# Query weights of a decode attention kernel: 448 rows spread evenly, 64 rows placed by DMA engine

## The chip, the cores and the metric

The kernel runs on one core of a Trainium2 chip. A core has TensorE (PE, with weight loads shown as PEld), VectorE (DVE), ScalarE (ACT), GpSimd (POOL) and SyncE (SP, which here only issues transfers), each with its own instruction queue run in order, and 16 DMA engines that move data between HBM and the on-chip memory of 128 partitions (SBUF). SP, ACT and POOL can issue DMAs; each queue's transfers are spread over the 16 DMA engines. The metric is device time in microseconds, the median of several runs.

## The reference: what is computed

One decode step, all in float32: a layer norm of `x`, a query projection, attention of 8 batches and 32 query heads over 8 cached key/value heads of 8192 positions, an output projection, and beside it a token-mixing MLP; the three are added.

```python
B, Sq, D = 8, 1, 512
Hq, Hkv, Sk, Dh = 32, 8, 8192, 128
xn = _layernorm(x, axis=-1)
q = (xn @ wq).reshape(B, Sq, Hq, Dh)            # wq: (512, 4096), 8.4 MB
k, v = repeated k_cache, v_cache                # each (8, 8, 8192, 128), 268 MB
p = softmax(q k^T * Dh ** -0.5)
attention = (p v).reshape(B, Sq, Hq * Dh) @ wo  # wo: (4096, 512), 8.4 MB
h = _layernorm(xn, axis=-1)
mixer = gelu(h * w1 + b1) summed over 1792 features with w2, + b2
out = x + attention + mixer
```

## The kernel before, in words

Caches and weights come to 553.7 MB, read once. They pass through a ring of five slots (`slots`, 32 KB per partition each, 4 MB in all per slot). `slot(n)` hands out the next n slots in turn. `load_next()` takes the next load of a fixed list: first the key and value heads of kv-head pairs (`load_duo`, 8 MB each: K0, V0, K1, V1, ... with i = pair and batch), then, from kv head 6 on, one head of one batch at a time (4 MB). All these loads are issued on SP's queue in that order; each waits until the slots it overwrites have been read. A load that spans slots 4 and 0 is issued as two transfers (V0 is the first such).

The order of work within an engine is the order of the program (`manual_schedule`); waits on semaphores between engines, and between a transfer and whoever reads or overwrites its target, are put in by the framework. Transfers from SP and ACT share eight completion counters in turn, those from POOL eight others: a transfer waits for the one that used its counter before it.

Start: `load_wq` (L88) reads all of `wq` into slots 0 and 1 as one transfer, four weight rows (64 KB) per partition. `load_next()` then issues K0 into slots 2 and 3 in four pieces and, after it, V0, whose first half goes into the free slot 4 and whose second half needs slot 0 and so the end of the projection. POOL issues `w1`, `b1`, `w2` and `b2` (L158 to L161), makes the identity matrix and clears `Z`, `PT` and `OTS` (L248 to L257). DVE builds small constant masks from the identity (L171 to L246; `fill_softmax`, `fill_place`, with scratch space in `early`), then does the layer norms and `yx = x + b2` into `macc` (L277), which waits for `b2`'s transfer. PE transposes `xn` (L282), puts `yx` into its place (L285), and then `q_project` (L297) does 32 matmuls: each group of four writes four 32-row groups of one PSUM tile. ACT copies the result, PE transposes it (L303), DVE stores it as `QT`.

Main loop (`duo_step`): DVE transposes the keys in place in 32x32 blocks (L480), PE forms scores (L491), a softmax runs over DVE, PE and ACT, and PE multiplies with the values (L523). Two halves of K are done one after the other; the first half's last matmul frees its slot, and `load_next()` issues the next K there. `load_wo(0)` is issued in step i = 2.

Of the kernel before, what the change touches and what calls it, by code (L numbers as in the profile page):

```python
# [10 lines left out]
ALU = mybir.AluOpType  # L11
# [29 lines left out]
PAD = 384  # L41


@with_exitstack
def attn_mixer_kernel(ctx: ExitStack, tc: tile.TileContext, x, kc, vc, wq, wo, w1, b1, w2, b2, out):
# [38 lines left out]
    WQ = []  # L84

    def load_wq():
        t = slot(2).rearrange("p s m -> p (s m)")
        nc.sync.dma_start(t, wq.rearrange("(p c) n -> p (c n)", c=NC))  # L88
        t = t.rearrange("p (c n) -> p c n", c=NC)
        WQ.extend(t[:, c, :] for c in range(NC))  # L90
# [57 lines left out]
    load_wq()  # L148
    early = one.tile([P, HB, 512], F32, name="ob")
    x_sb = early[:B, 0, :]  # L150
    nc.scalar.dma_start(x_sb, x.rearrange("b s d -> (b s) d"))
# [3 lines left out]
    b2t = const.tile([B, 1], F32, name="b2t")  # L155
    yrow = const.tile([W, D], F32, name="yrow")
    load_next()
    nc.gpsimd.dma_start(w1t, w1.rearrange("s (p c) -> p (s c)", p=P))  # L158
    nc.gpsimd.dma_start(b1t, b1.rearrange("(p c) -> p c", p=P))
    nc.gpsimd.dma_start(w2t, w2.rearrange("(p c) s -> p (c s)", p=P))  # L160
    nc.gpsimd.dma_start(b2t, bass.AP(tensor=b2.tensor, offset=b2.offset, ap=[[0, B], [1, 1]]))  # L161
# [3 lines left out]
    ident = const.tile([P, P], F32, name="ident")  # L165
    make_identity(nc, ident)

    oh32 = pad[:, 3 * NF:3 * NF + W]  # L170
# [19 lines left out]
    def fill_softmax(duo, tmp):  # L190
        tmp = tmp[:, :P]
        n = 2 if duo else 1
        rows = tmp[:, :n * REP].rearrange("p (s h) -> p s h", h=REP)
        nc.vector.tensor_reduce(rows, ident.rearrange("p (c s x h) -> p s h c x", c=NCH, s=n, h=REP), AX.XY, ALU.add)
        for s in range(n):
            nc.vector.tensor_scalar(hmask.rearrange("p (c s x h) -> p s c x h", c=NCH, s=n, h=REP)[:, s],
                                    rows[:, s].unsqueeze(1).unsqueeze(1).to_broadcast([P, NCH, B // n, REP]),
                                    1.0, 3.0e38, op0=ALU.subtract, op1=ALU.mult)
        if duo:
            nc.vector.memset(send, 0.0)  # L200
            for k in range(2):
                for a in range(NB):
                    o = a * W + a // 2 * HW
                    nc.vector.tensor_copy(send[:, k, o:o + HW].rearrange("p (c h) -> p c h", h=REP),
                                          ident.rearrange("p (c x h) -> p c x h", c=NCH, h=REP)[:, :, 2 * a + k, :])
        else:
            nc.vector.tensor_copy(send[:, 0, :].rearrange("p (x c h) -> p c x h", c=NCH, h=REP),
                                  ident.rearrange("p (c x h) -> p c x h", c=NCH, h=REP))

    def fill_place(duo, tmp):  # L210
        tmp = tmp[:, :P]
# [24 lines left out]
    fill_softmax(True, early[:, 2, :])  # L236
    fill_place(True, early[:, 3, :])
    epst = const.tile([B, 1], F32, name="epst")
    nc.vector.memset(epst, EPS)
# [8 lines left out]
    nc.gpsimd.memset(Z, 0.0)  # L248
    PT = []
    for k in range(NPT):  # L250
        t = const.tile([P, CH_T * W + W], F32, name=f"pt{k}")
        nc.gpsimd.memset(t, 0.0)
        PT.append(t)
    OTS = []
    for k in range(2):
        t = const.tile([P, REP, W], F32, name=f"ot{k}")
        nc.gpsimd.memset(t, 0.0)  # L257
        OTS.append(t)


    def layer_norm(dst, src):
        st = work.tile([B, 6], F32, name="st")
        nc.vector.bn_stats(st, src)
        mv = work.tile([B, 2], F32, name="mv")
        nc.vector.bn_aggr(mv, st)
        sd = work.tile([B, 1], F32, name="sd")
        nc.scalar.activation(sd, mv[:, 1:2], AF.Sqrt, bias=epst)
        rs = work.tile([B, 1], F32, name="rs")
        nc.vector.reciprocal(rs, sd)
        nc.vector.tensor_scalar(dst, src, mv[:, 0:1], rs, op0=ALU.subtract, op1=ALU.mult)  # L270

    xn = early[:B, 1, :]
    layer_norm(xn, x_sb)
# [4 lines left out]
    xnT = early[:, 2, P:2 * P].rearrange("p (c b) -> p c b", b=W)  # L278
    nc.vector.memset(xnT, 0.0)
    m = misc()  # L280
    for c in range(NC):
        nc.tensor.transpose(m[:, c * B:(c + 1) * B], xn[:, c::NC], ident[:B, :B])  # L282
    nc.vector.tensor_copy(xnT[:, :, :B], m[:, :NC * B].rearrange("p (c b) -> p c b", b=B))
# [7 lines left out]
    def q_project():  # L291
        for a in range(2):
            m = misc()
            for c in range(NC):
                for g in range(HKV // 2):
                    o = (a * HKV // 2 + g) * REP * DH
                    nc.tensor.matmul(m[g * W:(g + 1) * W, :], xnT[:, c, :], WQ[c][:, o:o + REP * DH],  # L297
                                     start=(c == 0), stop=(c == NC - 1))
# [3 lines left out]
            for r in range(REP):  # L302
                nc.tensor.transpose(mt[:, r * P:(r + 1) * P], q[:, r * DH:(r + 1) * DH], ident)  # L303
            nc.vector.tensor_copy(QT[:, a * HKV // 2:(a + 1) * HKV // 2].rearrange("p g b r -> p r g b"),
                                  mt.rearrange("p (r g b) -> p r g b", r=REP, b=W)[:, :, :, :B])
        WQ.clear()
# [293 lines left out]
    def duo_step(i):  # L600
# [27 lines left out]
        if b == 2:  # L628
# [150 lines left out]
```

## Time and profile before

| What | Value |
|---|---|
| median of 3 runs | 1292.99 us (1292.84 to 1293.36) |
| the profiled execution | 1293.02 us, span 1291.2 us |
| busy: PE, DVE, ACT, POOL | 923.2, 701.6, 233.0, 229.5 us |
| moved by DMA | 554.41 MB, mean 429 GB/s |
| first and last of 40 slices | 399 and 322 GB/s |
| chain that ended last | DMA 59%, PE 20%, DVE 19% |
| granted TensorE clock | 0.879 of full speed |

Times in the profile are in us from the span's start; a row of the timeline has start, duration, engine, line, operation, target and sources, and in brackets the idle time before it and what ended it. Rows of the chain of waits have start, duration and what the time went to. In rows of issues the last number is the time from issue to landing. The engine shown as SPq or ACTq is the queue that issues.

### The profile page before, as it was taken

The numbers are of one execution on the slowest core, as the hardware profiler recorded it, in microseconds if no ns is written. First come the engines' busy times: TensorE is split into PE (matmuls) and PEld (weight loads), VectorE is DVE, ScalarE is ACT, GpSimd is POOL, SyncE is SP. The second block draws the span as 40 slices with busy tenths as digits, with TensorE's granted clock in tenths as the row PEclk, the third lists the DMA queues.
The fourth block names the chain that finished last, engine by engine and source line by source line (L and its number), as shares of the span: only waits on it lengthen the run. The fifth ranks groups of instructions, "written<-read, shape, count | busy, mean of one in ns | idle before, by whom it ended". The sixth has DMA issues, their size and how long they took to land.

```text
span 1291.2 us, 11170 instructions
## 1 busy us (share of the span) xinstructions
PE 923.2 (72%) x4742; PEld 246.7 (19%) x4742; DVE 701.6 (54%) x581; ACT 233.0 (18%) x346; POOL 229.5 (18%) x247
## 2 busy tenths in 40 slices
PE   2766865866885876886768787688688674665778
PEld 0211211211221111211112121122112111111223
DVE  3544635644655633665445665346565745566575
ACT  0112220122121122121221221211222332310000
POOL 1022220222031222111221212211223311100000
PEclk9978997988998889898889988799897887878889
DMA  9999999999999999999999999999999999999997
GB/s 399 445 425 447 423 431 443 425 435 435 432 436 433 421 441 439 425 434 441 422 444 425 427 445 418 435 442 429 427 437 428 432 434 431 432 436 429 433 436 322
DMA packets 15925, 554.41 MB, mean 429 GB/s; under 512 B 1884, under 2 KB 1916, under 8 KB 2692
## 3 DMA queue, kind: packets, MB, share of 16 engines
q1 hardware_dynamic: 15732, 553.67, 99.4%
q8 instruction: 37, 0.61, 0.2%
q14 instruction: 12, 0.10, 0.0%
q0 software_dynamic: 128, 0.02, 0.0%
q10 hardware_dynamic: 16, 0.02, 0.0%
HBM read 553.69 MB, written 0.02 MB: 429 GB/s over the span
## 4 chain that ended last, share of the span: by engine, by line
DMA 59%; PE 20%; DVE 19%; ACT 1%; issue 1%; POOL 0%; SPq 0%; DVEq 0%; ACTq 0%; POOLq 0%
DMA raw<-in_A_k_cache_dram 54%; DVE raw L480 14%; PE acc L491 10%; DMA raw<-in_A_v_cache_dram 4%; DVE raw L336 3%; PE acc L414 3%; PE acc L523 3%; DMA b2t<-in_B_b_dram 2%; PE acc L347 1%; PE misc L511 1%; PE misc L297 1%; PE misc L540 1%; DVE mr L359 0%; ACT t2k L508 0%; DVE mr L500 0%
## 5 line engine op out<-in xcount | busy, mean ns | idle before, releaser
L491 PE MATMUL acc<-raw,z 128*32 128x512 f32 x1536 | 401.1, 642 | 188.6 <-DVE raw L480 183.2
L480 DVE STREAM_TRANSPOSE raw<-raw 128x2048 f32<-128x2048 f32 x192 | 424.1, 2274 | 170.8 <-DMA raw<-in_A_k_cache_dram 170.8
L575 POOL TENSOR_SCALAR g<-g,pad 128x512 f32<-128x512 f32 x112 | 77.5, 692 | 753.0 <-ACT g L574 753.0
L491 PEld LDWEIGHTS acc<-raw,z 128*32 128x32 f32 x1536 | 92.0, 116 | 496.4 <-issue 317.8
L523 PE MATMUL acc<-raw,pt 128*32 128x512 f32 x1536 | 181.5, 610 | 5.2 <-DMA raw<-in_A_v_cache_dram 5.2
L336 DVE STREAM_TRANSPOSE raw<-raw 128x2048 f32<-128x2048 f32 x64 | 145.6, 2293 | 60.7 <-DMA raw<-in_A_k_cache_dram 60.7
L576 POOL TENSOR_TENSOR macc<-macc,g 128x512 f32<-128x512 f32 x112 | 142.1, 1269 | 9.3
L574 ACT ACTIVATE g<-hb,pad 128x512 f32<-128x512 f32 x112 | 87.2, 778 | 147.6 <-POOL macc L576 125.4
L508 ACT ACTIVATE t2k<-acc,nb 128x512 f32<-128x512 f32 x24 | 16.5, 687 | 462.4 <-DVE nb L504 462.3
L347 PE MATMUL acc<-raw,z 128*32 128x512 f32 x512 | 82.2, 645 | 10.6 <-DVE raw L336 7.9
L511 PE MATMUL misc<-t2k,send 128*128 128x512 f32 x96 | 62.4, 785 | 33.5 <-ACT t2k L508 33.5
L414 PE MATMUL acc<-raw,pt 128*32 128x512 f32 x480 | 79.6, 803 | 0.0
L523 PEld LDWEIGHTS acc<-raw,pt 128*32 128x32 f32 x1536 | 48.0, 113 | 137.4 <-issue 106.7
L512 DVE STREAM_TRANSPOSE pt<-misc 128x512 f32<-128x512 f32 x48 | 34.4, 717 | 69.4 <-PE misc L511 67.7
L500 DVE TENSOR_REDUCE mr<-acc 128x1 f32<-128x512 f32 x24 | 16.6, 691 | 89.1 <-PE acc L491 89.1
L364 PE MATMUL misc<-ident,mr 128*128 128x128 f32 x16 | 6.5, 406 | 74.0 <-DVE mr L359 74.0
L574 ACT ACT_TABLE_LOAD x32 | 41.1, 1283 | 26.6 <-PE hb L566 26.1
L531 ACT COPY ob<-acc 128x512 f32<-128x512 f32 x24 | 14.0, 584 | 133.1 <-PE acc L523 133.1
L381 ACT ACTIVATE t2k<-acc,nb 128x512 f32<-128x512 f32 x16 | 11.0, 687 | 133.9 <-DVE nb L370 133.8
L347 PEld LDWEIGHTS acc<-raw,z 128*32 128x32 f32 x512 | 19.4, 116 | 62.7 <-issue 43.5
L636 ACT ACT_TABLE_LOAD x24 | 30.8, 1283 | 0.4
L540 PE MATMUL misc<-ob,pick 128*128 128x512 f32 x64 | 29.5, 603 | 0.4 <-ACT ob L531 0.4
(119 smaller groups left out, 334.6 us busy)
## 6 DMA issues: line engine op xcount, KB each, us to landing
raw<-in_A_k_cache_dram SPq DMA_DIRECT2D x26, 4096.0 KB, 28.6
raw<-in_A_v_cache_dram SPq DMA_DIRECT2D x25, 4096.0 KB, 28.1
raw<-in_A_k_cache_dram SPq DMA_DIRECT2D x4, 2048.0 KB, 33.3
wo<-in_A_wo_dram SPq DMA_DIRECT2D x7, 1024.0 KB, 28.8
raw<-in_A_v_cache_dram SPq DMA_DIRECT2D x3, 1024.0 KB, 21.8
raw<-in_A_v_cache_dram SPq DMA_DIRECT2D x2, 512.0 KB, 25.4
wo<-in_A_wo_dram SPq DMA_DIRECT2D x4, 256.0 KB, 16.3
raw<-in_A_v_cache_dram SPq DMA_DIRECT2D x19, 28.8
```

What stands on the lines that cost most here:

```text
L336: nc.vector.transpose(k, k)
L347: nc.tensor.matmul(S[i][c * W:(c + 1) * W, :].rearrange("p (t j) -> p t j", j=W), Z[:, q, b, REP:], k[:, c * CH_T:(c + 1) * CH_T, q * W:(q ...
L414: nc.tensor.matmul(O[i][j * W:(j + 1) * W, :].rearrange("p (c d) -> p c d", c=NCH), pt[:, t * W:(t + 1) * W], v[:, t], start=(t < NB), sto ...
L480: nc.vector.transpose(k, k)
L491: nc.tensor.matmul(SD[i][c * W:(c + 1) * W, :].rearrange("p (t j) -> p t j", j=W), Z[:, q, b, (1 - k) * REP:(1 - k) * REP + W], t[:, c * C ...
L511: nc.tensor.matmul(m, send[:, k, :], p, start=True, stop=True)
L512: nc.vector.transpose(PT[k][:, :CH_T * W], m)
L523: nc.tensor.matmul(OD[i][j * W:(j + 1) * W, :].rearrange("p (c d) -> p c d", c=NCH), PT[k][:, t * W:(t + 1) * W], v[:, t], start=(not k an ...
L540: nc.tensor.matmul(m.rearrange("p (b d) -> p b d", b=HB), pick[:, c, :], ob[:, :, c * DH:(c + 1) * DH], start=(c == 0), stop=(c == NCH - 1))
L574: nc.scalar.activation(g, hb, AF.Gelu_apprx_tanh, bias=b1t[:, j:j + 1], scale=w1t[:, j:j + 1])
L575: nc.gpsimd.tensor_scalar(g, g, w2t[:, j:j + 1], 1.0, op0=ALU.mult, op1=ALU.mult)
L576: nc.gpsimd.tensor_add(acc, acc, g)
```

## The change: what it does

The 512 rows of `wq` are no longer one transfer. The first 448 rows (D - WS with WJ = 14) lie as 14 pieces of 4 KB in each of the 128 partitions: `body`, 56 KB per partition in slots 0 and 1, loaded in two halves. The last 64 rows (WS), 16 KB each, go to chosen partitions of slot 4 (`extra`), one or two rows side by side (WE = 2); all else in `extra` is filled with zeros by DVE (3072 columns), POOL (2560) and ACT (2560) beforehand. [...] SP issues 28 of these rows and the last 16 columns of six and of four half rows; POOL issues the rest in six transfers with six dummy transfers of a few bytes between them (`pass_over`), one ahead of each.

Since a partition now holds pieces of different rows, `xn` is laid out to match: DVE copies it into `xg` and `xs` (42 small copies), PE transposes, DVE scatters the result into `lw` and `lx`, zero elsewhere. `q_project` has 44 matmuls instead of 32: 14 on the first half of `body`, 16 on `extra`, 14 on the second half.

Moved along: `x` and `b2` are issued first, on ACT's queue; `w1`, `b1`, `w2` are issued by POOL after the rows; `load_wo(0)` follows K0 on SP's queue; `Z`, `PT`, `OTS` are cleared by DVE; the scratch space of `fill_softmax` and `fill_place` moves from `early` to the rest of slot 1 (`spare`), as `lw` and `lx` now lie in `early`. V0 still goes to slots 4 and 0.

```diff
+    flat = wq.rearrange("d n -> (d n)")
+    body = slot(2).rearrange("p s m -> p (s m)")
+    extra = slots[:, RING - 1, :]
+    rows = flat[:P * WJ * WB].rearrange("(p m) -> p m", p=P)
+    half = WJ // 2 * WB
+    nc.sync.dma_start(body[:, :half], rows[:, :half])
+    spare = body[:, WJ * WB:]
+    nc.vector.memset(nil, 0.0)
+    nc.vector.memset(extra[:, :3072], 0.0)
+    nc.gpsimd.memset(extra[:, 3072:5632], 0.0)
+    nc.scalar.copy(extra[:, 5632:], nil.to_broadcast([P, WE * DR - 5632]))
...
+    def load_block(eng, p, n, r, d, hop, m=1):
+        to = extra[p:p + n * r, :m * DR].rearrange("p (e c) -> p e c", c=DR)
+        eng.dma_start(to, from_wq(d, [hop * DR, n], [DR, r * m]))
+        given.extend((p + i * r, r, d + i * hop, m) for i in range(n))
+
+    def load_steps(eng, p, step, n, d, hop, m=2, skip=1):
+        to = extra[p:p + (n - 1) * step + 1:step, :m * DR].rearrange("p (e c) -> p e c", c=DR)
+        eng.dma_start(to, from_wq(d, [hop * DR, n], [skip * DR, m]))
...
+    def pass_over(n):
+        at = 3 * NF + W + passed[0] // 2 * 4 + passed[0] % 2
+        passed[0] += 1
+        nc.gpsimd.dma_start(pad[:n, at:at + 3:2].unsqueeze(2), wq[:n, 0:3:2].unsqueeze(2))
+
+    D0 = D - WS
+    load_block(nc.sync, 0, 5, REP, D0, 6)
+    load_steps(nc.sync, W, REP, 3, D0 + 4, 6)
+    load_steps(nc.sync, W + 1, REP, 2, D0 + 60, 1, 1)
...
+    load_top(nc.sync, slice(DR - 16, DR))
+    load_halves(nc.sync, DR // 2 - 16, 16)
+    nc.sync.dma_start(body[:, half:WJ * WB], rows[:, half:])
+
+    def load_side():
+        pass_over(7)
+        load_block(nc.gpsimd, 60, 2, REP, D0 + 30, 10, 2)
+        pass_over(6)
+        load_top(nc.gpsimd, slice(0, DR - 16))
...
+        pass_over(7)
+        load_steps(nc.gpsimd, 28, 68, 2, D0 + 22, 1, 2, 6)
+        pass_over(6)
+        load_steps(nc.gpsimd, W + 2, 92, 2, D0 + 38, 1, 2, 13)
+        pass_over(6)
+        load_halves(nc.gpsimd, 0, DR // 2 - 16)
...
+        pass_over(6)
+        load_steps(nc.gpsimd, W + 3, 92, 2, D0 + 56, 1, 2, 2)
...
     load_next()
+    load_wo(0)
+    ident = const.tile([P, P], F32, name="ident")
+    make_identity(nc, ident)
+    load_side()
...
-    fill_softmax(True, early[:, 2, :])
-    fill_place(True, early[:, 3, :])
+    fill_softmax(True, spare[:, 7 * P:7 * P + HP])
+    fill_place(True, spare[:, 7 * P + HP:8 * P])
...
-    nc.gpsimd.memset(Z, 0.0)
+    nc.vector.memset(Z, 0.0)
...
+        part = [[(lw[:, j, :], body[:, j * WB:(j + 1) * WB]) for j in range(a * WJ // 2, (a + 1) * WJ // 2)] for a in range(2)]
+        part.insert(1, [(lx[:, j, :], extra[:, j * WB:(j + 1) * WB]) for j in range(WE * NB)])
...
-        if b == 2:
+        if g and b == 2:
             load_wo(2 * g)
```

What the built programs hold at three places. Names in brackets are the semaphores that the instruction waits for: DMAHW0 to 7 are the completion counters of transfers from SP and ACT, DMASW0 to 7 those from POOL, used in turn.

SP's queue at the start, now (before, row L88 and K0's four pieces stood first, without a wait, and V0's first half behind them, without a wait too):

```order
L100 DMA raw<-in_A_wq_dram 128x7168
L115 DMA raw<-in_A_wq_dram 20x1x4096 [waits DVE_49,Pool_49]
L120 DMA raw<-in_A_wq_dram 3x8192 [waits Activation_49]
L143 DMA raw<-in_A_wq_dram 128x7168 [waits DMAHW0_49]
L175 DMA raw<-in_A_k_cache_dram 128x4096 [waits DMAHW1_49]
L215 DMA wo<-in_A_wo_dram 128x2048 [waits DMAHW5_49]
L181 DMA raw<-in_A_v_cache_dram 128x8192 [waits DMASW7_49,DMASW5_49,DMAHW6_49,DMASW3_49,DMAHW7_49,DMASW1_49,PE_49]
L181 DMA raw<-in_A_v_cache_dram 128x8192 [waits DMAHW0_49,PE_49]
```

V0's first half (the first L181) now waits for PE, up to its last matmul on `extra`.

DVE, from the constants to the projection, before:

```order
L181 COPY rep<-ident 128x512
L194 TENSOR_REDUCE ob<-ident 128x8
L196 TENSOR_SCALAR hmask<-ob 128x4x16 [waits DVE_49]
L277 TENSOR_SCALAR macc<-ob,b2t 8x512 [waits DMASW3_49]
L304 COPY qt<-misc 128x4x32 [waits PE_49] x2
```

and now:

```order
L294 COPY rep<-ident 128x512
L306 TENSOR_REDUCE raw<-ident 128x8 [waits DMAHW4_49,DMASW7_49,DMAHW5_49,DMASW5_49,DMASW1_49]
L308 TENSOR_SCALAR hmask<-raw 128x4x16 [waits DVE_49]
L357 MEMSET z 128x1152
L361 MEMSET pt_257 128x544
L373 TENSOR_SCALAR macc<-ob,b2t 8x512 [waits DMAHW2_49]
L401 COPY qt<-misc 128x4x4x8 [waits PE_49] x2
```

The scratch space now lies in the ring's memory, and the framework makes its first write (L306) wait for transfers of rows into other places of that memory. DMASW1 is raised by POOL's block (`load_block`) and again by its half rows (`load_halves`); L306 waits for both.

PE around the projection, now, with POOL's own queue behind it:

```order
L375 MATMUL misc<-macc,ob 32x512 [waits DVE_49]
L391 MATMUL misc<-raw,ob 32x512 [waits DMAHW1_49]
L391 MATMUL misc<-raw,ob 32x512 x6
L391 MATMUL misc<-raw,ob 32x512 [waits DMAHW3_49,DMASW7_49,DMAHW4_49,DMASW5_49,DMAHW5_49,DMASW3_49,DMASW1_49]
```

```order
L126 DMA pad<-in_A_wq_dram 7x2x1
L115 DMA raw<-in_A_wq_dram 8x1x8192 [waits DVE_49,Activation_49]
L126 DMA pad<-in_A_wq_dram 6x2x1 [waits DMASW0_49]
L139 DMA raw<-in_A_wq_dram 2x2x2032 [waits DMASW1_49]
```

As before, the matmul on `macc` (L375, was L285) stands ahead of the projection, and `macc` waits for all of DVE's rows above it. POOL's half rows (L139) wait until its block has landed, since they use the same counter.

More of the change, by code (lines that the diff above doesn't have):

```diff
@@ L41 @@
 PAD = 384
+WJ = 14
+WB = 2 * REP * DH
+WS = D - P * WJ // NB
+WV = 2
+WE = 2
 @with_exitstack
@@ L83, in attn_mixer_kernel @@
     order[at], order[at + 1] = order[at + 1], order[at]
[L84 to L90, printed above, removed]
+    early = one.tile([P, HB, 512], F32, name="ob")
+    x_sb = early[:B, 0, :]
+    nc.scalar.dma_start(x_sb, x.rearrange("b s d -> (b s) d"))
+    b2t = const.tile([B, 1], F32, name="b2t")
@@ new lines, in attn_mixer_kernel @@
+    xn = early[:B, 1, :]
+    layer_norm(xn, x_sb)
+    cls = const.tile([P, WV], F32, name="cls")
+    nc.vector.tensor_reduce(cls, ident.rearrange("p (u v) -> p v u", v=WV), AX.X, ALU.add)
+    NE = max(WJ * v % NB + WJ - 1 for v in range(WV)) // NB + 1
+    xg = spare[:B, :NE * P].rearrange("b (e p) -> b e p", e=NE)
+    xs = spare[:B, NE * P:(NE + WE) * P].rearrange("b (e p) -> b e p", e=WE)
+    nc.vector.memset(xs, 0.0)
+    US = WJ * WV // NB
+    for v in range(WV):
+        for e in range(NE):
+            d = WJ * v // NB + e
+            nc.vector.tensor_copy(xg[:, e, v::WV], xn[:, d:d + US * (P // WV - 1) + 1:US])
@@ new lines, in attn_mixer_kernel @@
+    for p, r, d, m in given:
+        e = slice(0, m) if m > 0 else slice(-m, 1 - m)
+        n = max(m, 1)
+        nc.vector.tensor_copy(xs[:, e, p:p + r], xn[:, d:d + r * n].rearrange("b (k e) -> b e k", e=n))
+    lw = early[:, 2, :WJ * W].rearrange("p (j x) -> p j x", x=W)
+    lx = early[:, 3, P:P + WE * NB * W].rearrange("p (j x) -> p j x", x=W)
+    nc.vector.memset(lw, 0.0)
+    nc.vector.memset(lx, 0.0)
+    m = misc()
+    for e in range(NE):
+        nc.tensor.transpose(m[:, e * B:(e + 1) * B], xg[:, e], ident[:B, :B])
@@ L302, in q_project @@
             for r in range(REP):
[L303 to L306, printed above, removed]
+                nc.tensor.matmul(mt[:, r * W:(r + 1) * W], q[:, r * DH:(r + 1) * DH], oh32, start=True, stop=True)
+            nc.vector.tensor_copy(QT[:, a::2].rearrange("p g b r -> p r g b"),
+                                  mt[:, :REP * W].rearrange("p (r g b) -> p r g b", r=REP, b=B))
         load_next()
```

90 lines of the change are left out of this document (52 added, 38 removed).

## The prediction

> **What bounds the kernel now.** I read the page first, then a table of stretches, then the chain of waits and the timelines of the first 50 us. The page's lines on the 16 DMA engines (the span in 40 slices, then two queues: packets, MB, share of 16 engines):
>
> ```profile
> DMA  9999999999999999999999999999999999999997
> q1 hardware_dynamic: 15732, 553.67, 99.4%
> q8 instruction: 37, 0.61, 0.2%
> ```
>
> The DMA engines are busy from the first slice to the last. The busy time by stretch says how fast they then are (last two columns: DMA share, GB/s):
>
> ```profile
> 45.00:960.00 915.00, 675.06 (x3249) 173.67 (x3247) 490.95 (x339) 167.88 (x239) 183.55 (x190) 0.89 1.00 434
> ```
>
> 434 GB/s with nothing idle is 27.1 GB/s for each of 16 engines: 2.42 us for 64 KB, and by the same rate 1.21 for 32 KB, 1.06 for 28 KB, 0.60 for 16 KB. So time is lost only in two ways: some DMA engine has more to move than the others, or the queue runs empty. The chain of waits at the start and the issues on SP's and GpSimd's queues show how far off the second is:
>
> ```profile
> 3.10 20.16 DMA b2t<-in_B_b_dram
> 23.28 0.49 DVE macc L277
> 23.81 1.91 PE misc L285 x2
> 25.72 5.98 PE misc L297 x32
> ...
> 33.02 3.61 PE misc L297 x32
> ...
> 38.38 8.71 DVE raw L480 x4
> 47.09 0.04 issue
> 47.14 3.63 PE acc L491 x16
> 50.77 0.02 issue
> 50.79 31.53 DMA raw<-in_A_k_cache_dram
> ...
> 82.34 17.68 DVE raw L480 x8
> ```
>
> ```profile
> 0.74 0.39 SPq L88 DMA_DIRECT2D raw<-in_A_wq_dram  x1
> 1.20 2.38 SPq L105 DMA_DIRECT2D raw<-in_A_k_cache_dram  x4
> 3.62 31.63 SPq L111 DMA_DIRECT2D raw<-in_A_v_cache_dram  x2
> 50.79 0.33 SPq L105 DMA_DIRECT2D raw<-in_A_k_cache_dram  x1
> 70.84 0.33 SPq L105 DMA_DIRECT2D raw<-in_A_v_cache_dram  x1
> 94.94 0.33 SPq L105 DMA_DIRECT2D raw<-in_A_k_cache_dram  x1
> ```
>
> Weights, K0 and half of V0 (20 MB) are queued by 4 us and last until about 50; V0's second half is issued at 34.9 (3.62 + 31.63, less its own 0.33), when the queue has some 15 us left. The late start of the query projection (25.7, held by the 20 us of `b2t`) therefore costs nothing before.
>
> **The change, its aim.** Eight DMA engines get 64 of the 512 weight rows and eight get none. What it is worth: the 37 packets of q8, 16 KB each (0.61 MB), took 0.2% of 16 x 1291 us, some 41 us (31 to 52 by the rounding). If they all fall on the eight engines without rows, these end 41/8 = 5.2 us late against a mean of 2.6. Taking four rows from each (half a row per partition on eight partitions) removes 4 x 0.60 = 2.4 us: an end of 1293.0 - 2.4 = 1290.6 at best. No view names a packet's engine.
>
> **The change, its start.** V0's first half now goes into the slot that holds the spread rows (`extra`), so SP cannot issue it before PE has read them. Queued until then are weights 8.39, K0 8.39 and `wo` 1.05 MB. The weights landed at 0.74 + 22.3, as this row of the issues has it:
>
> ```profile
> raw<-in_A_wq_dram SPq DMA_DIRECT2D x1, 22.3
> ```
>
> K0 takes 8.39/0.434 = 19.3 us more and `wo` 2.4: the queue is empty at 44.7 on the mean engine, at about 42 on those without rows and 49 on those with eleven. (Moving `wo` adds this 2.4 here and takes it away at 150 us: nothing in sum.) The five small SP transfers and K0's new waits for completion counters cost nothing while 8 us of `body` stand queued ahead of them; without that cover each issue would cost its 0.4 to 0.6 us.
>
> When has PE read `extra`? The orders above give the path: DVE's L306 waits for GpSimd's half rows (counter DMASW1, raised by the block and then by the halves), DVE then goes through all its constants to `macc` (L373), PE's L375 waits for `macc`, and the projection stands behind L375. Four terms.
>
> (1) *GpSimd's rows.* GpSimd's packets take turns with SP's on each DMA engine:
>
> ```profile
> 1.26 0.78 POOL L158 DMA_DIRECT2D pad<-in_B_w_dram  x1 [0.82 <-POOLq L766]
> 2.04 0.55 POOL L159 DMA_DIRECT2D pad<-in_B_b_dram  x1
> 3.10 0.53 POOL L161 DMA_DIRECT2D b2t<-in_B_b_dram  x1
> DMA to landing us min/median/max: 9.5/13.7/18.1
> ```
>
> (The last row is that of the tile `pad`.) They land at 10.8, 15.7, 20.7, and `b2t` at 23.3: two 64 KB rows (4.84 us) for each transfer, one that its data waits behind and one that its completion waits behind. The first: 9.5 = 0.78 + 4.84 + about 3.9, so about 3 us from the end of an issue until it stands in the queue, the rest waiting for a turn. The block waits for ACT's fill of `extra` (two issues from 0.74, a table load, 2560 columns):
>
> ```profile
> 0.74 0.59 ACTq L151 DMA_DIRECT2D ob<-in_A_x_dram  x1
> 1.36 1.28 ACT L267 ACT_TABLE_LOAD   x1 [1.36 <-PEq L766]
> 31.72 0.58 ACT L300 COPY t2k<-misc 128x512 f32<-128x512 f32 x1 [18.81 <-PE misc L297]
> ```
>
> 0.74 + 2 x 0.6 + 1.28 + five times 0.58 at most is 6.1, less 0.9 if the fixed part of a copy is paid once; I take 5.4. Issued at 5.9, queued at 9. Its four 32 KB rows on one engine alternate with 28 KB of `body`: 4 x (1.21 + 1.06) = 9.1, the completion 1.06 more: 19. The halves wait for that counter, are issued at 19.5 and queued by 23, behind what GpSimd has issued since: three completions (3.2, to 22.4), two rows of 16 KB (3.3, to 25.7), four completions that now wait only for K0's 16 KB packets (2.4, to 28.1); then the halves 1.8 and their completion 0.6: 30.5. I take 30. Ends: 23 if completions took no turn, 49 if a row went out in pieces of 4 KB.
>
> (2) *DVE from L306 to `macc`.* The same operations before, first and last:
>
> ```profile
> 5.89 0.37 DVE L194 TENSOR_REDUCE ob<-ident 128x8 f32<-128x128 f32 x1
> ...
> 9.62 0.16 DVE L246 COPY ob<-ident 8x8 f32<-8x8 f32 x1
> ...
> 11.70 0.68 DVE L263 BATCH_NORM_STATS2 st<-ob 8x6 f32<-8x512 f32 x1
> ...
> 13.13 0.53 DVE L270 TENSOR_SCALAR hn<-ob,mv,rs 8x512 f32<-8x512 f32 x1
> ```
>
> 3.9 for the constants, 2.0 for the second layer norm, 0.5 for `macc`, and five memsets that were GpSimd's:
>
> ```profile
> 6.60 0.27 DVE L200 MEMSET send<- 128x256 f32 x1
> 4.15 1.05 POOL L248 MEMSET z<- 128x1152 f32 x1
> 6.41 0.44 POOL L257 MEMSET ot<- 128x128 f32 x2
> ```
>
> 2496 columns, 2.7 us on GpSimd (4.15 to 6.85), 2.6 at DVE's 0.27 for 256. Sum 9.0: `macc` at 39. (GpSimd's share was hidden; DVE's stands on the path.)
>
> (3) *PE.* L285's 1.9 us, then 30 of 44 projection matmuls up to the last on `extra`. 32 took 5.98 + 3.61, so 9.0: to 50. (The twelve added ones stand behind or within; K0's transposes start near 55 instead of 38.4 and K1's issue, 12.4 later as before, near 67, while V0 is still moving until 71: the ring takes that up, with 2 us to spare.)
>
> (4) *From issue to movement.* The weights' 22.3 less eight rows of 2.42 leave 2.9 for start and landing; 1 to 2.9, I take 1.9. V0 starts at 52 on every engine.
>
> Against 44.7 the mean engine idles 7.4 us. All engines now restart together, so the head start given to eight of them is gone and q8's packets, nearly all after 52, make the same spread as before. What ends the kernel stays:
>
> ```profile
> 1259.46 25.35 DMA raw<-in_A_v_cache_dram
> ```
>
> the last piece of V at 1284.8, 6.4 us before the span's end. The profiled execution took 1293.02 (span 1291.2 and 1.8 around it), the median 1292.99, so they can be used alike: 1293.0 + 7.4, rounded, **1300.4 us**. By the ends of term (1), the other terms kept: at 23 nothing is lost, at 49 it is 26.
>
> [...]
>
> **The rivals.** *The cover holds.* The rows land by 23 (completions riding with data), V0 is issued by about 44.7 and the slowest engine never idles. For it: 42 to 49 us are queued; against it: the spacing of 4.9 us between `pad`'s landings. Then 1290.6 at best, but the ring gives some back: K2 is issued at 94.94, V1, issued at 70.84 behind K1 (landed 82.3, 50.79 + 31.53), is through at 82.3 + 19.3 = 101.6, and an engine more than 101.6 - 94.9 - 1.9 = 4.8 us ahead of the slowest runs dry. Eleven rows (counted by groups of four partitions) against none is 6.65: 1.8 of the 2.4 is lost again. 1292.4, not slower; it decides if V0's issue comes before 45.
>
> [...]
>
> *Pieces of 4 KB.* The block needs 32 turns and is done only as K0 ends; halves at 49: 1293 + 26 = 1319.
>
> [...]
>
> **How the numbers follow.** Forecast (1298 to 1304) 0.58, cover holds 0.20, one turn 0.09, elsewhere 0.07, small pieces 0.06. This kernel's measurement tells about 0.2% (2.6 us) from no change. Of "cover holds" 0.07 lies below 1290.4 and 0.13 within; the rest, 0.80, is slower. The likeliest case alone runs from 1297 to 1304; to leave out no more than two in ten the range takes the upper part of "cover holds" and the lower of what is beyond: 1292 to 1306.
>
> **What would show it.** A row of DVE at L306 that waits some 15 us for a wq transfer and ends near 30; L373 near 39; L391 from 41; V0's issue (SP, L181) near 50 behind PE; the second DMA slice (32 to 65 us) at 7 or 8 instead of 9, its GB/s falling by about a quarter, everything later shifted by one constant. A projection before 35 and full slices would make the prediction wrong at term (1); a right V0 issue with a smaller shift, at the claim that the restart wipes out the balance.

## The result and the profile after

The changed kernel takes **1307.66 us** (median; 1307.21 to 1308.62), the kernel before 1293.12 beside it on the same chip: a ratio of 1.0114 (95% interval 1.0101 to 1.0126). The forecast was 1300.4 (1292 to 1306): slower, as forecast, but by 14.5 us instead of 7.4, and outside the range. The profiled execution has a span of 1305.7 us.

The page of the changed kernel: the 40 slices of DMA busy time and of GB/s, and GpSimd's queue (packets, MB, share of 16 engines):

```profile
DMA  9699999999999999999999999999999999999997
GB/s 391 258 444 420 432 436 441 422 442 432 425 441 434 424 444 426 430 436 444 417 445 426 429 429 447 422 442 434 423 438 429 432 430 434 433 429 432 432 431 325
q0 software_dynamic: 672, 0.61, 0.1%
```

The second slice is the one that lost its work. A table of three stretches, first of the kernel before, then of the changed one (the last two columns are DMA share and GB/s):

```profile
0.00:35.00 35.00, 11.09 (x62) 3.13 (x66) 10.13 (x48) 2.46 (x4) 6.23 (x16) 1.00 0.95 401
35.00:60.00 25.00, 19.84 (x100) 4.95 (x92) 18.30 (x10) 1.61 (x5) 0.00 (x0) 0.93 1.02 440
300.00:1200.00 900.00, 655.06 (x3236) 172.14 (x3237) 492.31 (x376) 180.78 (x266) 175.68 (x182) 0.87 1.00 433
```

```profile
0.00:35.00 35.00, 0.99 (x6) 0.83 (x6) 11.01 (x72) 5.18 (x4) 11.61 (x22) 1.00 0.95 393
35.00:60.00 25.00, 14.29 (x93) 3.75 (x93) 8.43 (x39) 1.01 (x3) 0.52 (x1) 1.00 0.52 208
300.00:1200.00 900.00, 652.01 (x3232) 172.76 (x3232) 494.34 (x372) 180.11 (x264) 175.61 (x182) 0.87 1.00 433
```

(401 - 393) GB/s over 35 us is 0.6 us of transfer at 434 GB/s; (440 - 208) over 25 us is 13.4 us. Together 14.0, and from 300 us on the two run alike at 433. So nearly all of the loss is made before 60 us, and it stays.

What made it, in the changed kernel's chain of waits (start, duration, what):

```profile
5.59 12.97 DMA raw<-in_A_wq_dram
18.56 0.28 issue
18.85 18.07 DMA raw<-in_A_wq_dram
36.94 0.40 DVE raw L306
...
45.26 0.41 DVE macc L373
45.71 1.91 PE misc L375 x2
47.62 12.20 PE misc L391 x88
...
74.90 23.97 DMA raw<-in_A_k_cache_dram
98.90 17.68 DVE raw L576 x8
...
1273.52 25.75 DMA raw<-in_A_v_cache_dram
```

GpSimd's block of rows goes out at 5.59, its half rows (issued when the block has landed) at 18.85; they land 18.1 us later, and only then does VectorE's reduce L306 run. The last piece of V lands at 1299.27 (1273.52 + 25.75), 14.46 later than before. On SP's queue V0's first half is issued in the middle of the projection, when no DMA engine has had work for 7 us or more:

```profile
56.44 2.07 SPq L181 DMA_DIRECT2D raw<-in_A_v_cache_dram  x2
```

The trace also holds a record of every DMA packet: queue, start, duration and size. It doesn't name the packet's engine, but in these traces a packet begins as the one before it on its engine ends (in the changed kernel most often from 4 ns before to 3 ns after), so that idle engines can be counted. By these records 16 stretches of work end between 42.1 and 49.1 us (45.0 on average), one on each engine, eight of them by 43.6 and eight from 45.1 on, and V0 begins between 57.4 and 58.1 on all of them.

### The profile page after: what moved, and what is told of

It is laid out like the page before. It is cut to its first block, busy times and chain, and to the rows that moved or that the text cites. A ratio compares the mean times of both kernels' runs of the same rounds, so it can differ in the third digit from the quotient of the medians.

```text
span 1305.7 us, 11325 instructions
## 1 busy us (share of the span) xinstructions
PE 919.7 (70%) x4776; PEld 251.4 (19%) x4776; DVE 711.4 (54%) x645; ACT 236.7 (18%) x348; POOL 235.4 (18%) x254
## 3 DMA queue, kind: packets, MB, share of 16 engines
q1 hardware_dynamic: 15924, 553.08, 98.3%
## 4 chain that ended last, share of the span: by engine, by line
DMA 59%; PE 20%; DVE 18%; ACT 1%; issue 1%; POOL 0%; SPq 0%; ACTq 0%; DVEq 0%
DMA raw<-in_A_k_cache_dram 52%; DVE raw L576 14%; PE acc L587 10%; DMA raw<-in_A_v_cache_dram 4%; DVE raw L432 3%; PE acc L619 3%; PE acc L510 2%; DMA raw<-in_A_wq_dram 2%; PE acc L443 1%; PE misc L607 1%; PE misc L391 1%; PE misc L636 1%; DVE mr L455 0%; ACT t2k L604 0%; DVE mr L596 0%
## 5 line engine op out<-in xcount | busy, mean ns | idle before, releaser
L587 PEld LDWEIGHTS acc<-raw,z 128*32 128x32 f32 x1536 | 95.2, 117 | 485.7 <-issue 308.8
L619 PE MATMUL acc<-raw,pt 128*32 128x512 f32 x1536 | 180.2, 607 | 6.1 <-DMA raw<-in_A_v_cache_dram 6.1
L510 PE MATMUL acc<-raw,pt 128*32 128x512 f32 x480 | 75.5, 766 | 0.0
L670 ACT ACT_TABLE_LOAD x32 | 41.1, 1283 | 23.3 <-PE hb L662 22.8
L443 PEld LDWEIGHTS acc<-raw,z 128*32 128x32 f32 x512 | 19.4, 116 | 62.5 <-issue 43.4
## 6 DMA issues: line engine op xcount, KB each, us to landing
wo<-in_A_wo_dram SPq DMA_DIRECT2D x7, 1024.0 KB, 17.8
wo<-in_A_wo_dram SPq DMA_DIRECT2D x4, 256.0 KB, 25.9
```

The lines of the kernel that those rows point to most:

```text
L443: nc.tensor.matmul(S[i][c * W:(c + 1) * W, :].rearrange("p (t j) -> p t j", j=W), Z[:, q, b, REP:], k[:, c * CH_T:(c + 1) * CH_T, q * W:(q ...
L510: nc.tensor.matmul(O[i][j * W:(j + 1) * W, :].rearrange("p (c d) -> p c d", c=NCH), pt[:, t * W:(t + 1) * W], v[:, t], start=(t < NB), sto ...
L587: nc.tensor.matmul(SD[i][c * W:(c + 1) * W, :].rearrange("p (t j) -> p t j", j=W), Z[:, q, b, (1 - k) * REP:(1 - k) * REP + W], t[:, c * C ...
L619: nc.tensor.matmul(OD[i][j * W:(j + 1) * W, :].rearrange("p (c d) -> p c d", c=NCH), PT[k][:, t * W:(t + 1) * W], v[:, t], start=(not k an ...
L670: nc.scalar.activation(g, hb, AF.Gelu_apprx_tanh, bias=b1t[:, j:j + 1], scale=w1t[:, j:j + 1])
```

## The experiments

Each ratio is to the kernel before, run beside it on the same chip.

**Where the wait comes from.** The scratch space of the two fill functions in a buffer of its own, so that VectorE writes nothing in the ring while rows are on their way there:

```diff
-    fill_softmax(True, spare[:, 7 * P:7 * P + HP])
-    fill_place(True, spare[:, 7 * P + HP:8 * P])
+    scratch = big()
+    fill_softmax(True, scratch[:, :HP])
+    fill_place(True, scratch[:, HP:P])
```

> Only the scratch space of fill_softmax and fill_place leaves the ring's memory (a t2k buffer instead). Theory (V0's issue is late because DVE waits at L306 for GpSimd's half rows): DVE no longer waits, yx is placed by about 26 us, and the projection now waits only for the last GpSimd row, which by the turns should land near 39.5; 16 cold matmuls of 0.37 later V0 is issued near 45.5 instead of 56.4, and the DMA engines without rows idle some 2.6 us past 43.9 instead of 13.5. Time 1296 us (1295 to 1297.5). Rival (the loss lies in the small packets or in the uneven load themselves, not in the wait): within 3 us of the changed kernel, 1305 to 1308.

Measured: 1296.33 us, ratio 1.0026 (1.0016 to 1.0036). Its timeline of PE and of SP's queue:

```profile
23.30 1.91 PE L376 MATMUL misc<-macc,ob 8*32 8x512 f32 x2 [11.68 <-DVE macc L374]
25.14 5.41 PE L392 MATMUL misc<-raw,ob 128*32 128x512 f32 x28
39.49 8.49 PE L392 MATMUL misc<-raw,ob 128*32 128x512 f32 x60 [8.94 <-DMA raw<-in_A_wq_dram]
44.61 2.85 SPq L181 DMA_DIRECT2D raw<-in_A_v_cache_dram  x2
```

As expected: the matmul on `macc` runs at 23.3 again instead of 45.7, and PE itself now waits for GpSimd's last rows, until 39.5. This change of three lines takes back 11.3 of 14.7 us. So the wait of one small reduce was the price, not the work of VectorE or PE around it.

**Why the rows are so late: smaller turns.** K0 in eight pieces of 8 KB per partition instead of four of 16 KB, so that each turn that a packet of GpSimd's waits for is half as long:

```diff
-            n = 1 if to is VP or i else 4
+            n = 1 if to is VP or i else 8
```

> K0 is loaded in eight pieces of 8 KB per partition instead of four of 16 KB; nothing else. Theory (a GpSimd packet waits for one packet of SP's queue each time, so its delay goes with the size of that packet): the turns after about 23 us are half as long, the half rows land near 32.3 instead of 36.9, V0 is issued near 51.8, time 1303.1 us (1302 to 1304.5). Rival (the delay is GpSimd's own descriptor work or a share by time): half rows unchanged within 1 us, 1307 to 1308.5.

Measured: 1303.72 us, ratio 1.0086 (1.0072 to 1.0100). The issue of the half rows (KB, us from issue to landing) and VectorE's wait for them, in the changed kernel, and here:

```profile
raw<-in_A_wq_dram POOLq DMA_DIRECT2D x1, 31.8 KB, 18.1
36.94 0.39 DVE L306 TENSOR_REDUCE raw<-ident 128x8 f32<-128x128 f32 x1 [22.33 <-DMA raw<-in_A_wq_dram]
```

```profile
raw<-in_A_wq_dram POOLq DMA_DIRECT2D x1, 31.8 KB, 13.2
32.40 0.39 DVE L306 TENSOR_REDUCE raw<-ident 128x8 f32<-128x128 f32 x1 [17.78 <-DMA raw<-in_A_wq_dram]
```

The rows wait for turns, and what counts is the length of the other queue's packets; the wait of L306 ends at 32.4, as expected. The packet records show the turns themselves: in the changed kernel, on an engine that carries half rows, every packet of GpSimd's from 22.5 to 36 us, of 4 bytes or of 16 KB, is followed by one packet of SP's.

**Fewer packets.** The six rows for partitions 92 to 94, all on one DMA engine by the packet records of the changed kernel, replaced by a transfer of one value on the same completion counter, which leaves out six weight rows:

```diff
-        load_top(nc.gpsimd, slice(0, DR - 16))
+        nc.gpsimd.dma_start(pad[:1, 3 * NF + W + 20:3 * NF + W + 21], wq[:1, :1])
```

> GpSimd's transfer of six 16 KB rows to partitions 92 to 94 is replaced by one of a single value on the same counter, so six weight rows are missing from the projection (all else is computed). Theory (every GpSimd transfer takes as many turns on each of the 16 DMA engines as it has packets on its busiest one, filled with 4-byte packets): five turns fewer on all engines, the half rows land near 33.9 instead of 36.9, V0 is issued near 53.4, time 1304.6 us (1303.5 to 1305.5), and GpSimd's queue shows 672 - 80 = 592 packets. Rival (the six packets load only their own engine, as my prediction counted): half rows within 1 us of 36.9, 1307 to 1308, packets 667.

Measured: 1307.99 us, ratio 1.0117 (1.0103 to 1.0131). The page's row of the queue, the issue of the half rows, and PE's projection in the timeline:

```profile
q0 software_dynamic: 592, 0.52, 0.1%
```

```profile
raw<-in_A_wq_dram POOLq DMA_DIRECT2D x1, 31.8 KB, 16.0
```

```profile
46.80 13.12 PE L391 MATMUL misc<-raw,ob 128*32 128x512 f32 x88
```

The packets are what the theory counts: five fewer on each of 16 engines (672 - 80 = 592), though the rows left out were one engine's alone. The time isn't what it expected. The half rows came 2.1 us sooner after their issue (3.0 were expected), but the block before them landed 1.3 us later, for a reason I have not found, and the 0.8 us that was left went into PE: its 88 records took 13.1 instead of 12.3 us (more on this below). By the packet records the run then loses another 1.1 us, which the changed kernel doesn't: V1 is issued 20.2 us after K1, and 13 engines stand still from about 97 us until 97.3 to 98.3. So the packet count is the theory's and the time the rival's (1307 to 1308): this run alone shows the count, not the cost.

So the same theory was tried with a larger lever: the same transfers, packets and engines, but the six rows last in the queue instead of third (two of the dummies are over 14 rows, meant to keep every row on its engine). The half rows no longer share the block's counter and are issued at 9.0 instead of 18.85, but they still stand in the queue behind the block:

```diff
+        pass_over(14)
+        load_steps(nc.gpsimd, 28, 68, 2, D0 + 22, 1, 2, 6)
...
+        load_halves(nc.gpsimd, 0, DR // 2 - 16)
...
+        pass_over(14)
+        load_top(nc.gpsimd, slice(0, DR - 16))
```

> The change with the same transfers in another order on GpSimd's queue: the six rows (partitions 92 to 94, one DMA engine) come last instead of third, and two of the dummies are over 14 rows so that every row still falls on the same engine and q0 moves the same 672 packets; the half rows now stand eighth and no longer wait for the block's counter. Theory (on every DMA engine each GpSimd transfer takes as many turns as its busiest engine): six rows, their completion and one dummy with its own (9 turns of 0.6 us) no longer stand ahead of the half rows, so the reduce at L306 ends its wait at 31.9 instead of 36.9, V0 is issued at 51.3, the stretch from 10 to 28 us keeps its 415 GB/s, and the time is 1302.5 us (1301.2 to 1304.3). Rival (rows cost turns only on the engines that carry them; the six rows are on another engine than the half rows): the wait ends within 1 us of 36.9 and the time stays above 1306.5 us.

Measured: 1304.86 us, ratio 1.0086 (1.0069 to 1.0103). Its queue has 672 packets again, and its timeline shows on VectorE and SP:

```profile
32.16 0.39 DVE L306 TENSOR_REDUCE raw<-ident 128x8 f32<-128x128 f32 x1 [17.56 <-DMA raw<-in_A_wq_dram]
52.36 2.07 SPq L181 DMA_DIRECT2D raw<-in_A_v_cache_dram  x2
71.16 0.33 SPq L175 DMA_DIRECT2D raw<-in_A_k_cache_dram  x1
91.38 0.33 SPq L175 DMA_DIRECT2D raw<-in_A_v_cache_dram  x1
```

The wait ends at 32.16 (31.9 expected, 36.9 if rows cost turns only on the engine that carries them): rows on *one* engine had held up half rows on *others*, nine turns, 4.8 us. Their earlier issue can't be what did it, since in the changed kernel GpSimd's packets ahead of them leave no gap on their engine from 22.5 us on. The time is 0.6 us above the range that was expected. V0 goes out 4.1 us earlier, and by 60 us 4.0 us are won (counted over the trace's packet records, as the bytes moved by then). But V1 is issued 20.2 us after K1 (91.38 and 71.16), and K1's 8.39 MB take 19.3 us to move at 434 GB/s; in the changed kernel V1 came 17.8 us after K1:

```profile
74.90 0.33 SPq L175 DMA_DIRECT2D raw<-in_A_k_cache_dram  x1
92.69 0.33 SPq L175 DMA_DIRECT2D raw<-in_A_v_cache_dram  x1
```

So eight of the engines run out of work a second time, at about 93 us and until 94.2 to 94.7, and between 90 and 100 us 1.5 us are lost again, where the changed kernel loses 0.1 (with K0 in eight pieces it is 1.7).

**The moved parts alone.** All 512 rows even, nothing in slot 4, no rows from GpSimd; everything else that the change moved stays where it put it, but for the scratch space, which has a buffer of its own:

```diff
-WJ = 14
+WJ = 16
...
-    load_side()
...
-        part.insert(1, [(lx[:, j, :], extra[:, j * WB:(j + 1) * WB]) for j in range(WE * NB)])
```

> All 512 weight rows lie evenly again (16 pieces of 4 KB per partition, in two halves), nothing goes into slot 4 and GpSimd issues no weight rows; what the change moved along stays: x and b2 first on ScalarE's queue, wo(0) behind K0, the clearing of Z, PT and OTS by VectorE, the new layout of xn, and the scratch space in a buffer of its own. Theory (only the rows in slot 4 cost something): V0's first half is issued before 20 us again, all 40 DMA slices stand at 9, GpSimd's queue moves about 100 packets, and the time is that before, 1293.0 us (1292.3 to 1293.8). Rival (some 1 to 2 us of the loss lie in the moved parts, VectorE's added work or the split of the weights): 1294.3 us or more.

Measured: 1293.15 us, ratio 1.0001 (0.9992 to 1.0010). `x`, `b2`, `wo(0)`, the memsets and the new layout cost nothing that can be measured; all of the loss belongs to the rows in slot 4 and the waits for them.

**What the balance is worth when V0 is in time.** Own scratch space and K0 in eight pieces together:

> Both edits: scratch space out of the ring, K0 in eight pieces. Theory: the last GpSimd row lands near 33.7, V0 is issued near 40 before any DMA engine runs dry at 42, so the start costs nothing and what is left is the balance itself. If the ring gives most of it back (an engine more than about 4.8 us ahead of the slowest runs dry near 100 us): 1292.4 to 1293.5 us. Rival (the balance holds to the end): 1290.6 to 1291.2 us. If V0 is still late: 1294 or more.

Measured: 1295.24 us, ratio 1.0016 (1.0007 to 1.0025), span 1292.9:

```profile
38.93 2.84 SPq L181 DMA_DIRECT2D raw<-in_A_v_cache_dram  x2
```

V0 is issued before any engine is idle, and yet the kernel is 2.25 us above the one before. Neither expectation holds. By the bytes moved (again by packet records, in us at 434 GB/s) it lies 0.9 us behind the kernel before by 35 us, without an idle engine. (GpSimd's rows and small packets are the likely price, not `body`'s smaller pieces: the last version below loads its first half in the same 28 KB pieces and is 0.0 behind by then. No run takes the two apart further.) It stays so until 100 us, grows to 1.7 by 106, as six engines stand still from about 101 to 102 us, and to 2.4 by 300, and comes back to 2.0 at the end. The start costs 1.0, and the ring takes 1.4 more; the balance returns at most half a microsecond at the end, where the last piece of V lands 1.4 later than before (1286.25 and 1284.81).

**Without the dummies.** The dummy transfers cost turns; first taken out of the changed kernel, then out of the version just shown:

```diff
         passed[0] += 1
-        nc.gpsimd.dma_start(pad[:n, at:at + 3:2].unsqueeze(2), wq[:n, 0:3:2].unsqueeze(2))
```

> The change as it is, without the six dummy transfers ahead of GpSimd's rows; where these rows fall is then left to the order of the queue, and the half rows no longer wait for the block's counter. Theory (every GpSimd transfer puts packets on all 16 DMA engines, and each takes a turn with SP's): q0 moves 672 - 6 x 32 = 480 packets; four dummies of two turns each (4 x 2 x 0.6 us) no longer stand ahead of the half rows, so the reduce at L305 ends its wait at 32.2 instead of 36.9 (29 if the rows then fall on different engines one after the other, 36 if all on the same two), V0 is issued near 51.6, and whatever the rows' placement is now, it is forgotten when all engines restart together: 1302.9 us (1299.5 to 1304.5). Rival 1 (the dummies' packets of a few bytes cost nothing): the wait ends at 36.9, 1307.7 us. Rival 2 (the placement that the dummies steer is worth some 2 us even here): V0 near 51.6 but 1305 us or more.

> The version with the scratch space in a buffer of its own and K0 in eight pieces, which came out at 1295.2 us, without the six dummy transfers. Theory (the uneven rows buy little, since engines that run ahead stand still again near 100 us): with 192 packets of a few bytes fewer on GpSimd's queue the start is some 0.3 us quicker, the placement is another one and matters little, 1294.9 us (1294.0 to 1295.8). Rival (the placement by dummies is worth 1 us or more at the end, and hidden in 1295.2): 1296.3 us or more.

Measured: 1307.00 us, ratio 1.0108 (1.0094 to 1.0121), and 1304.48 us, ratio 1.0088 (1.0074 to 1.0101). Only the 480 packets came as expected. Both theories fall: in the first the wait ends at 36.68 instead of 32.2, and the times are near those of the rivals (1307.7; 1296.3 or more), but for another reason than theirs. The stretch from 10 to 28 us in the changed kernel, then in these two:

```profile
10.00:28.00 18.00, 0.38 (x2) 0.29 (x2) 4.53 (x41) 0.00 (x0) 2.32 (x5) 1.00 1.00 415
```

```profile
10.00:28.00 18.00, 0.38 (x2) 0.29 (x2) 4.52 (x41) 0.00 (x0) 1.06 (x2) 1.00 1.01 262
```

```profile
10.00:28.00 18.00, 5.08 (x20) 1.24 (x23) 12.87 (x80) 0.29 (x1) 1.60 (x3) 1.00 1.02 265
100.00:110.00 10.00, 9.66 (x34) 1.90 (x32) 10.00 (x5) 0.00 (x0) 0.00 (x0) 0.79 0.79 341
```

The DMA engines are busy all the while (share 1.01 and 1.02) and move 262 GB/s instead of 415: 6.3 us lost, before anything waits for the rows. (The table's last row is another loss: the queue of the second version runs dry after 106 us, which by 150 us has cost 3 us more.) By the packet records each packet of the first stretch simply lasts longer: a 28 KB piece of `body` that begins in it 1.75 and 1.73 us on average instead of 1.08. In the first version none of them took less than 1.21 us, so every engine is slowed. The dummies are meant to decide which engine brings each row; that this has to be the engine which also brings the pieces of `body` for the same partitions was the author's assumption, to whose failing the prediction gave a chance of 0.07 ("elsewhere"). No view names a packet's engine or its partition, so this was put to a test.

**Rows on another engine, everything else alike.** The version with the own scratch space and K0 in eight pieces, with the first dummy over eight rows instead of seven, which is meant to send every row of GpSimd's through an engine one further on:

```diff
     def load_side():
-        pass_over(7)
+        pass_over(8)
```

> The version with the scratch space in a buffer of its own and K0 in eight pieces (1295.2 us), with the first dummy transfer over eight rows instead of seven: the same number of transfers and packets in the same order, but each of GpSimd's row transfers begins one DMA engine further on, so that its rows go through engines other than those that bring the body's pieces into these partitions. Theory (a row that another engine writes into a partition group stands against the group's own engine and slows all of them, which is what cost 7 us without the dummies): 672 packets on q0 as before, between 10 and 28 us the DMA moves 250 to 320 GB/s instead of some 420, the first slice falls from 387 to about 305 GB/s, 1302.3 us (1300 to 1305.5). Rival (without the dummies it was the rows' coming all at once that cost the 7 us, not where they fell): 1295.2 us (1294.3 to 1296.2).

Measured: 1304.73 us, ratio 1.0089 (1.0076 to 1.0103). Its stretch, after that of the version it is made from:

```profile
10.00:28.00 18.00, 5.09 (x20) 1.24 (x23) 12.87 (x80) 0.29 (x1) 2.86 (x5) 1.00 1.00 412
```

```profile
10.00:28.00 18.00, 5.08 (x20) 1.24 (x23) 12.87 (x80) 0.29 (x1) 1.70 (x3) 1.00 1.01 326
```

The queue's 672 packets and their order are the same, the rate falls to 326 GB/s, and the time is 9.5 us longer: it is where the rows fall, not that they come all at once. (The first slice, at 332 GB/s, fell less than to the 305 that I expected; by the packet records the version falls behind the kernel before by another 0.6 us between 28 and 35 us and as much between 35 and 40.) Why rows on other engines slow all 16 (in the version without dummies `body`'s pieces took 1.21 us at least between 10 and 28 us, where the changed kernel has 1.06) no run shows.

**The rows by SP alone.** 480 rows even and 32 rows, all issued by SP, none by GpSimd, with the scratch space in a buffer of its own and K0 in four pieces; first as one block of 20 rows that lie one behind the other in memory and two transfers of six, then with the 20 rows read in another order, five groups of rows five apart:

```diff
-WJ = 14
+WJ = 15
...
-    load_block(nc.sync, 0, 5, REP, D0, 6)
+    load_block(nc.sync, 0, 5, REP, D0, 4)
```

```diff
-    load_block(nc.sync, 0, 5, REP, D0, 4)
+    nc.sync.dma_start(extra[:5 * REP, :DR], from_wq(D0, [DR, 5], [5 * DR, REP]))
```

> 480 rows even (15 pieces of 4 KB per partition) and 32 rows by SP alone into slot 4: 8 each through engines 0, 1 and 2, 4 each through engines 3 and 4; GpSimd issues no rows and no dummies; scratch space in a buffer of its own, K0 in four pieces. Theory (it is GpSimd's packets that cost the start, and the uneven rows pay where no engine runs more than some 4.8 us ahead): V0's first half is issued by 36 us, the slices all stand at 9, every engine but five has two rows (1.2 us) less than before, so 1293.0 - 1.2 + 0.2 for the smaller packets = 1292.0 us (1291.2 to 1292.9). Rival (a head start given at 20 us is worn off again near 100 us, whoever issues the rows): 1293.2 us or more.

> As the version before it (480 rows even, 32 rows by SP alone), but the 20 rows of its first transfer are read in another order (five groups of four rows that lie five apart), so that the transfer has a slowest dimension of 5 and not of 20 and is dealt to engines 0 to 4, four partitions each, the ones whose groups they write, instead of two partitions each to ten engines. Theory (the 1.3 us that the version before lost between 10 and 20 us came from rows in partition groups of other engines): nothing is lost there, the stretch from 10 to 28 us moves 412 GB/s or more, and what remains is the gain of the two rows less on eleven engines: 1292.2 us (1291.4 to 1293.0). Rival (an uneven start is worn off whoever brings it, and the 1.3 us are the price of the small transfers between the two halves): 1293.5 us or more.

Measured: 1294.34 us, ratio 1.0010 (1.0001 to 1.0019), and 1294.60 us, ratio 1.0011 (1.0002 to 1.0020). Two stretches and the issue of K2, of the first, then of the second:

```profile
10.00:28.00 18.00, 4.38 (x17) 1.25 (x19) 14.06 (x85) 0.29 (x1) 0.53 (x1) 1.00 1.00 398
100.00:110.00 10.00, 7.56 (x31) 1.84 (x31) 5.51 (x6) 0.27 (x1) 0.00 (x0) 1.00 1.01 439
99.45 0.33 SPq L173 DMA_DIRECT2D raw<-in_A_k_cache_dram  x1
```

```profile
10.00:28.00 18.00, 3.52 (x13) 1.05 (x16) 14.90 (x100) 0.29 (x1) 0.52 (x1) 1.00 1.00 429
100.00:110.00 10.00, 7.56 (x31) 1.84 (x31) 5.43 (x6) 0.35 (x1) 0.00 (x0) 1.00 1.00 400
99.37 0.33 SPq L174 DMA_DIRECT2D raw<-in_A_k_cache_dram  x1
```

In the first, the block went out as two rows on each of ten engines, by the packet records, not as the expectation has it: 398 GB/s. With the same rows read in another order they are four rows on each of five engines: 429, or 31 GB/s over 18 us = 1.3 us won back. Which engines these are, and which partitions they write otherwise, no record shows. The second has thus no loss at the start at all, and still it gains nothing: near 105 us it moves 400 GB/s where the first moves 439. Seven engines have run out of work between 100.8 and 101.4 us, and K2, issued at 99.4 in both, reaches them from 101.2 to 102.1 only; in the first, whose rows lie on twice as many engines and so less unevenly, none runs dry. By the packet records it is 0.0 us behind the kernel before at 100 us, 1.0 at 110 and 1.9 at 300. The two times don't differ beyond their spread. So the rival was right in its main part: a head start given at 20 us is worn off within 300. Its other part, that the 1.3 us are the price of the small transfers, falls.

No version beats the kernel before; the nearest is the one with even rows, at the same time.

## Why the prediction was wrong

The direction was right, and so was the path: rows, reduce, `macc`, projection, V0. The step that failed is the size of its first term. By the steps of the prediction:

- **Term (1), GpSimd's rows, is the step that was mis-sized**: 30 was taken, 36.9 measured. Its first half held: the block was issued at 5.6 (5.9), landed at 18.6 (19), the half rows went out at 18.85 (19.5). ACT's fill of `extra`, 2.9 us at most by the prediction, took 2.32. What failed is the count of what stood ahead of the half rows: "three completions", "two rows of 16 KB", "four completions", twelve turns with the half rows themselves. It counted rows only on the engine that carries them. In fact every GpSimd transfer puts as many packets on each of the 16 engines as its busiest engine has: the six rows, the dummies and the rows for partitions 34 and 126 count as well, 24 turns instead of twelve. By the packet records the last piece of `body` ends at 25.9; seven turns against 28 KB pieces before it (7.4 us from 18.5) and seventeen against K0's 16 KB after it (11.0 us to 36.9) make the 24. Shown by the version with the six rows last (36.9 becomes 32.2) and by K0 in eight pieces (32.4); the packet counts of 672, 592 and 480 agree with it. The 6.9 us of this term are made smaller by the next three: V0 begins 5.4 us later than the 52 that was forecast.
- **Term (2)**: 9.0 from L306 to `macc`, measured 8.7 (36.94 to 45.67). **Term (3)**: 10.9 for L375 and 30 of 44 matmuls, measured 10.7 (45.71 to 56.44). **Term (4)**: 1.9 from issue to movement, measured 1.0 (56.44 to 57.4).
- **The queue's end**: empty at 44.7 on average, from 42 to 49; measured 45.0, from 42.1 to 49.1: the 7.0 us between are eleven rows of 0.61 us and a little more. From then to the first packet of V0 at 57.4 it is 12.4 us instead of 7.4.
- **What was left out**: the start itself. While GpSimd's rows and little packets were under way, 0.8 us were lost by 40 us; the restart, where the engines begin one after the other (57.4 to 58.1) and with a slower packet (1.5 to 2.1 us for 32 KB, then 1.21), took another 0.7, and some 0.5 came later. With 12.4 that makes 14.4 of the 14.5 to 14.7 us.
- **The balance**: "the head start is gone" at the restart held (all engines begin V0 within 0.7 us). That the ring takes back 1.8 of 2.4 where the cover holds was nearly met in size: 1.4, but only 0.7 of it near 102 us, where it was expected. And "the cover holds" was priced at 1292.4 and came out at 1295.24, since the start cost 1.0 that it did not have, and at most 0.5 of the balance was still there at the end. No run changed q8's packets, so whether they are what makes the engines end unevenly stays open.
- **The rivals**: "one turn" (0.09) falls: packets of GpSimd and SP alternate one by one, as the packet records and K0 in smaller pieces (32.4 instead of 36.9) show. "Pieces of 4 KB" falls too: the block landed at 18.6, and its rows are packets of 32 KB. What "elsewhere" (0.07) stands for cost some 9 us when it was put to the test (1304.5 and 1304.7 against 1295.2).
- **In the profile**: the predicted signs came, L306 waiting for a wq transfer (22.3 us, not 15), V0 behind PE, one constant shift; the second slice stands at 6 rather than 7 or 8, and its GB/s fell by 42% rather than a quarter.

## What to carry over

Before a side queue is given rows to bring, count its packets per DMA engine as if each transfer ran on all of them, times the length of the main queue's packets: here 24 turns instead of the 12 counted, 36.9 us instead of 30. Put the first write into memory on which transfers are still under way behind the work that doesn't need it: three changed lines were worth 11 us here. An uneven start couldn't balance here what came later, since the ring let no engine run far ahead: of the versions with rows by SP alone the second was 0.0 us behind the kernel before at 100 us and 1.9 at 300.

## What the hardware showed

- **Packets on all engines.** In these runs a GpSimd transfer on one or two DMA engines shows as packets of 4 bytes on the others, as many as the busiest has, and from 22.5 to 36 us of the changed kernel each takes its turn with one of SP's packets, 0.61 us for 16 KB. Six rows on one engine are 96 packets; a value of 4 bytes in their place 16 (672 and 592).
- **Rows on other engines.** 36 rows of 16 KB (0.59 MB), no longer steered by the dummies, took the rate of all 16 engines from 415 to 262 GB/s for 18 us; with the first dummy over eight rows instead of seven it went from 412 to 326. Of SP's transfers the same 20 rows lay on ten engines when read as one run of memory, 398 GB/s from 10 to 28 us, and on five when read as five groups, 429.
- **PE's first microseconds.** The projection runs at half pace at first, although the granted clock stands at 1.00. In the kernel before its first 16 matmuls (32 records) took 5.99 us and the next 16 3.64; the 0.37 us of a "cold" matmul in an expectation is that first pace, 5.98 us over 16. In the changed kernel (busy us and records of L391 in two stretches):

```profile
45.00:51.00 6.00, 3.45 (x20) 0.82 (x23) 1.00 0.19 81
51.40:58.00 6.60, 6.60 (x66) 2.07 (x60) 1.00 0.27 77
```

20 records in 3.45 us, then 66 in 6.6 us. By the matmuls' start times four take 0.85 us until 5.5 us after PE's first matmul (L375) and 0.43 us from then on; without the six rows it was 7.2 us, with K0 in eight pieces 6.4, in the kernel before 6.5. That is how a start 0.8 us earlier came to nothing there. Why the pace changes no run shows.
